# Two weight loads of a cached-attention decode kernel: a quarter of each as 8-row loads from GpSimd's queue to partitions 64 to 127

## The chip, the cores and the metric

The kernel runs on one core of a Trainium2 chip. The metric is device microseconds of one execution; the time of a version is the median of its runs. Everything is in 32-bit floats.

## The reference

Two layers, each a grouped-query attention over a long cache for one new token, followed by a small mixer over the channels; the same weights and the same cache serve both layers. Two batch rows, 32 query heads on 8 key/value heads, 32,768 cached positions, head size 128.

```python
q = (x @ wq)...                                   # x: (2, 1, 512) after a layer norm
scores = jnp.einsum("bhqd,bhkd->bhqk", q, k) * (Dh ** -0.5)
p = _softmax(scores, axis=-1)
o = jnp.einsum("bhqk,bhkd->bhqd", p, v)
...
x = x + _A_ref(_layernorm(x), k_cache, v_cache, wq, wo)
x = x + _B_ref(_layernorm(x), w1, b1, w2, b2)     # mixer: b2 + w2 . gelu(w1 * norm + b1) on each channel
x = x + _A_ref(_layernorm(x), k_cache, v_cache, wq, wo)
x = x + _B_ref(_layernorm(x), w1, b1, w2, b2)
```

## The kernel before

A unit is one (layer, batch row, key/value head): 32 units, each with 8 chunks of K and 8 of V, 2 MB a chunk. For each unit TensorE forms the scores of its four query heads against K (L426), ScalarE the exponentials (L466), and TensorE the weighted sums of V (L581). One key/value head is a "keeper": much of its cache stays in memory from layer 0 to layer 1.

All of K, V and the weights come through SyncE's queue into one large tile, `mem`, cut into 13 cells of 16 KB a partition and a rest of five slots of 2 KB. Cells 0 to 8 (0 to 10 around the change of layer) hold K and V in a ring, cells 9 to 12 hold weights. A list of loads, `stream`, sorted by key, sets the order of the loads and of the matmuls; one step of it is one chunk. The function `at(time, f, ...)` hangs other work on steps of this stream: `make_q` some 6 steps ahead of a unit's K, `load_weights` 10 ahead, and so on. SyncE issues a load when the buffer's last readers and its last load are done, and each engine runs its own list of instructions in order.

Weights are loaded for two heads at once: `wqo[k]` holds for each partition the four query tiles (512 columns each, one for each block of 128 input channels `d`) and the four output tiles of both heads, 4 MB. `load_weights` (L115 to 118) brings them as one load of 128 rows; seven such loads are in the program, and the pair with number 1 (heads 2 and 3) is loaded twice, once in each layer. `q_products` (L340) multiplies the normalised input `xnT[:, d]` with query tile `d`, four products for each query, all into one bank.

`spot()` (L302) hands out scratch slots of 512 columns, eight of them in turn, all in cell 8. GpSimd computes a power now and then (L271, L685, L871) and issues no load.

Of the kernel before, what the change touches and what calls it, by code (L numbers as in the profile page):

```python
# [13 lines left out]
P = 128  # L14
CK = 4096
# [5 lines left out]
RING = 3  # L21
# [7 lines left out]
REST = 5  # L29
IN_PSUM = (4, 5, 3)  # L30
KEPT_Q = 4
RESIDENT = (5, 7)
TWO_HEADS = ((0, 1), (2, 3), (4, 6), RESIDENT)
FOLLOWS = {2: (2.2, -0.9, -0.8, -0.7, 3.5, -0.6, -0.5, -0.4), 5: (3.05, 0.1, 0.2, 0.3, 5.1, 3.1, 3.2, 3.3)}
PIECES = (32, 16, 8, 4, 4)
THIN = 16
QT = 4
# [7 lines left out]
def gqa_mixer_kernel(ctx: ExitStack, tc: tile.TileContext, x, kt, v, wqo, cols, out):  # L45
# [17 lines left out]
    nc = tc.nc  # L63
    B, D = out.shape
# [4 lines left out]
    R = wqo.shape[2] // (4 * D)  # L69
    DT = D // P  # L70
    FT = (cols.shape[1] - 1) // 4
# [13 lines left out]

    NP = 28 + 32 * 2
    widths = dict(x=B * DT, xn=B * DT, q=KEPT_Q * R, cols=4 * FT + 1, ident=P, one=1, half=1, selg=R * QT)
    widths |= dict(selh=R, mask=QT, others=B, oz=2 * R * B, qpads=NP, unit=2 * 16, ln=16 + 2 * FT)
    small_sb = const.tile([P, sum(widths.values())], F32, name="small_sb")
    sm, w0 = {}, 0  # L90
    for name, w in widths.items():
# [6 lines left out]
    W = wqo.shape[2] // 4  # L98
    assert CK == 2 * W
    WCELL0, WCELLS = RING * RING, 4  # L100
    heads = list(range(HKV))
    passing = [h for h in heads if h not in RESIDENT]
    home = {}
    mem = const.tile([P, (WCELL0 + WCELLS) * CK + REST * QT * DH], F32, name="mem")

    def cells(k, m=1):
        return mem[:, k * CK : (k + m) * CK]

    def wq_at(h):
        return cells(home[h])[:, :W].rearrange("p (t c) -> p t c", t=DT)  # L110

    def wo_at(h):
        return cells(home[h])[:, W:].rearrange("p (t c) -> p t c", t=R)

    def load_weights(k, cell):  # L115
        for j in range(2):
            home[TWO_HEADS[k][j]] = cell + j
        nc.sync.dma_start(cells(cell, 2), wqo[k])


    busy = [0] * 2 * (WCELL0 + WCELLS + 1)
    now = [0]
# [72 lines left out]
    ident = sm["ident"]  # L195
# [31 lines left out]
    rows = kept[-1]  # L227
# [52 lines left out]
    N1 = len(units) - 1  # L280
# [5 lines left out]
    N3 = len(units) - 1  # L286
# [7 lines left out]
    xnT = sm["xn"].rearrange("p (d b) -> p d b", b=B)  # L294
# [5 lines left out]
    spots = [0]  # L300

    def spot():  # L302

        spots[0] += 1
        return cells(RING * RING - 1)[:, spots[0] % (CK // D) * D :][:, :D]

    def to_columns(key):

# [24 lines left out]
    def q_products(n, *ds):  # L333

        layer, b, h = unit_of(n)
        m = 1 if partner(n) is None else B
        for d in ds:
            if d == 0:
                q_ps[n] = bcast if N1 < n <= N3 + 2 else kept[0]
            nc.tensor.matmul(  # L340
                q_ps[n][:m, :],
                xnT[:, d, b : b + m],
                wq_at(h)[:, d, :],
                start=(d == 0),
                stop=(d == DT - 1),
            )

    def make_q(n, step, place=None):

# [339 lines left out]
    ln = sm["ln"]  # L689
# [52 lines left out]
    def last_mixer(n):  # L742
# [185 lines left out]
    kbeg, k_done, vbeg, v_done, vend_of, v_from, v_to, brings, starts, t = {}, {}, {}, {}, {}, {}, {}, [], [], 0  # L928
# [13 lines left out]
    def at(time, f, *a, rank=1):  # L942
        done.setdefault(time, []).append((rank, f, a))

    HC = NCH // HALVES
    opens = {two[0]: k for k, two in enumerate(TWO_HEADS)}
    mixed = {}
    for n in range(NU):
        layer, b, h = unit_of(n)
# [19 lines left out]
                assert max(v_done[n - 2, c] for c in range(HC)) <= q2  # L969
        if n and h in opens and (units[n] == (0, 0, h) or h in passing and units[n] == (1, 0, h)):  # L970
            at(kbeg[n] - (7 if n == N3 + 2 else 10), load_weights, opens[h], WCELL0 + opens[h] % 2 * 2)
        if n in (N1 + 1, N2 + 1):
            at(kend - 0.5, turn_scores, n, 0, rank=2)
            at(kend, q_products, n + 1, 0)
            at(kend, max_1, n)
            at(kend, q_products, n + 1, 1)
            at(kend, max_2, n)
            at(kend, exponentials_at_once, n, 0)
            at(kend, q_products, n + 1, 2, 3)
            t1 = kend + 2  # L980
            assert mixed[units[n - 1][:2]] == kend == kbeg[n + 1] - 2
            at(t1, turn_scores, n, 1, rank=2)
            at(t1, exponentials_at_once, n, 1, rank=2)
            at(t1 + 1, sums, n)
            assert t1 + 1 < v_done[n, HC] - 1
        else:
            t1 = max(kend + 2, ahead + (2 if urgent else 4))
            e = kend if N1 < n <= N3 else kend + 2
            at(max(kend, e - 1), max_1, n)
            at(e, max_2, n)  # L990
            t0 = max(k_done[n, HC - 1], *(v_done[n - 1, c] for c in range(HC) if n), 0)
            if n in (N2, N3):
                t0 = max(t0, kbeg[n + 1] - 3)
            at(t0, turn_scores, n, 0)
            at(e, exponentials, n, 0)
            if n == NU - 1:
                t1 = ahead
                assert t1 >= kend + 2 and vbeg[n] == ahead
            at(t1, turn_scores, n, 1)
            at(t1, exponentials, n, 1)  # L1000
# [74 lines left out]
    t = 0  # L1075
# [11 lines left out]
    assert not done, sorted(done)  # L1087


def _layout(A_x, A_k_cache, A_v_cache, A_wq, A_wo, B_w1, B_b1, B_w2, B_b2):  # L1090

    import numpy as np

    B, HKV, SK, DH = A_k_cache.shape
    D = A_x.shape[-1]
    n = SK // CK


    keys = np.arange(SK).reshape(n, CK)
    for c0, m in GROUPS:  # L1100
        keys[c0 : c0 + m] = keys[c0 : c0 + m].reshape(P, m, CK // P).transpose(1, 0, 2).reshape(m, CK)
    k = keys.reshape(n // PACK, PACK // 2, 2, NG, 32, JT // QT, QT // SUB, SUB)
# [11 lines left out]
    return {  # L1114
        "x": np.ascontiguousarray(A_x.reshape(B * (D // P), P).T),
        "kt": kt,
        "v": A_v_cache.reshape(B * HKV, SK * DH),
        "wqo": np.stack([np.concatenate([wqo[h] for h in two], axis=1) for two in TWO_HEADS]),
        "cols": np.concatenate(cols, axis=1),
    }  # L1120

# [24 lines left out]
```

## Time and profile before

| | us |
|---|---|
| median of 3 runs (lowest to highest) | 2491.31 (2490.64 to 2491.49) |
| the profiled execution, its own time | 2490.09 |
| its span | 2488.0 |
| TensorE busy | 1371.4 (55%) |
| VectorE, ScalarE, GpSimd busy | 244.9, 187.7, 4.9 |
| bytes read from HBM | 1061.19 MB, 427 GB/s over the span |

The profile page cuts the span into 40 slices of 62.2 us; its DMA row gives the busy share of the 16 DMA engines in tenths, its GB/s row what they moved. Section 3 lists queues: q1 is SyncE's, q10 ScalarE's, q8 and q14 fetch instructions and tables. A table of stretches gives for each stretch the busy time of each engine, then the granted share of TensorE's clock, the DMA share (the mean over 16 engines; packets count where they are recorded, so single rows can pass 1.00) and GB/s. No view names a single DMA engine.

### The profile page before, as it was taken

How to read it: one execution, taken by the hardware profiler on the slowest of the kernel's cores; microseconds unless marked ns; L12 is line 12 of the kernel's file. 1: busy time of each engine (PE TensorE's matmuls, PEld its weight loads, DVE VectorE, ACT ScalarE, POOL GpSimd, SP SyncE). 2: the span in 40 equal slices, each digit the busy share in tenths (PEclk: the TensorE clock that was granted, in tenths of full speed). 3: DMA queues.
4: the chain of work that ended last, by engine and by line, in shares of the span. 5: the costliest groups of instructions: out<-in, count | busy, mean ns of one | idle time of the engine just before them, and what ended most of it. 6: DMA issues, size and time to landing. Idle time of an engine off the chain costs nothing.

```text
span 2488.0 us, 20543 instructions
## 1 busy us (share of the span) xinstructions
PE 1371.4 (55%) x9302; PEld 376.2 (15%) x9302; DVE 244.9 (10%) x643; ACT 187.7 (8%) x554; POOL 4.9 (0%) x17
## 2 busy tenths in 40 slices
PE   4544445544545454657677665455455465455546
PEld 1111111111111111111121121111111111111112
DVE  1000000000000000003113110000000000010002
ACT  0000000000000000002012000000000000011002
POOL 0000000000000000000000000000000000000000
PEclk8777767876777777778888887777678677777878
DMA  9999999999999999999999999999999999999996
GB/s 421 437 432 428 433 436 430 434 435 427 436 436 432 426 436 431 427 431 407 433 427 417 428 432 432 438 430 431 432 428 438 428 429 435 431 434 431 432 431 291
DMA packets 30336, 1062.51 MB, mean 427 GB/s; under 512 B 3621, under 2 KB 3625, under 8 KB 4266
## 3 DMA queue, kind: packets, MB, share of 16 engines
q1 hardware_dynamic: 29960, 1061.17, 99.1%
q8 instruction: 73, 1.20, 0.2%
q14 instruction: 13, 0.11, 0.0%
q10 hardware_dynamic: 290, 0.04, 0.0%
HBM read 1061.19 MB, written 0.00 MB: 427 GB/s over the span
## 4 chain that ended last, share of the span: by engine, by line
DMA 73%; PE 25%; DVE 1%; issue 0%; another core or an unknown queue 0%; ACT 0%; SPq 0%; POOL 0%; ACTq 0%
DMA mem<-in_v_dram 64%; PE acc L581 20%; DMA mem<-in_kt_dram 9%; PE scores L426 3%; PE small L612 0%; PE small L455 0%; PE small L449 0%; PE bcast L340 0%; ACT S L466 0%; PE small L642 0%; PE kept L246 0%; PE kept L792 0%; PE bcast L672 0%; DVE S L551 0%
## 5 line engine op out<-in xcount | busy, mean ns | idle before, releaser
L426 PE MATMUL scores<-mem,small_sb 128*32 128x512 f32 x4096 | 631.7, 736 | 605.4 <-DMA mem<-in_kt_dram 605.2
L581 PE MATMUL acc<-mem,S 128*16 128x512 f32 x4088 | 596.8, 723 | 457.1 <-DMA mem<-in_v_dram 447.7
L426 PEld LDWEIGHTS scores<-mem,small_sb 128*32 128x32 f32 x4096 | 150.0, 129 | 988.7 <-issue 903.7
L466 ACT ACTIVATE S<-S,small_sb 128x128 f32<-128x128 f32 x240 | 123.4, 517 | 2107.9 <-DVE small_sb L457 1556.9
L581 PEld LDWEIGHTS acc<-mem,S 128*16 128x16 f32 x4088 | 132.6, 109 | 810.8 <-issue 664.4
L441 DVE TENSOR_REDUCE small_sb<-scores 128x1 f32<-128x512 f32 x64 | 44.2, 691 | 819.5 <-PE scores L426 819.5
L461 DVE STREAM_TRANSPOSE S<-scores 128x512 f32<-128x512 f32 x64 | 45.5, 710 | 116.0 <-PE acc L581 116.0
L340 PE MATMUL kept<-mem,small_sb 128*2 128x512 f32 x104 | 51.1, 617 | 1.7 <-DVE small_sb L274 1.7
L466 ACT ACTIVATION_READ_ACCUMULATOR S<-S,small_sb 128x1 f32 x240 | 44.7, 186 | 0.0
L246 PE MATMUL kept<-mem,small_sb 128*1 128x512 f32 (+1 forms) x236 | 42.4, 598 | 2.6 <-ACT mem L835 2.4
L451 DVE TENSOR_REDUCE small_sb<-small 1x4 f32<-1x128 f32 x32 | 8.9, 279 | 277.7 <-PE small L449 277.7
L614 DVE RECIPROCAL small_sb<-small 128x4 f32<-128x4 f32 x32 | 5.9, 185 | 304.6 <-PE small L612 304.6
L623 DVE TENSOR_TENSOR small_sb<-small,small_sb 128x4 f32<-128x4 f32 x31 | 5.1, 164 | 295.8 <-PE small L621 295.8
L551 DVE SCALAR_TENSOR_TENSOR S<-acc,small_sb,S 128x128 f32<-128x128 f32 x93 | 32.6, 351 | 3.3
L835 ACT ACTIVATE S<-bcast,small_sb 128x512 f32<-128x512 f32 x28 | 21.5, 777 | 87.2 <-DVE small_sb L704 85.1
L366 PE MATMUL small<-small_sb,mem 2*128 2x2 f32 x112 | 15.5, 256 | 17.9 <-DVE mem L362 17.9
L549 DVE TENSOR_SCALAR S<-acc,small_sb 128x128 f32<-128x128 f32 x31 | 10.8, 350 | 147.3 <-PE acc L581 147.3
L621 PEld LDWEIGHTS small<-small_sb,S 128*128 128x128 f32 x62 | 12.7, 258 | 48.8 <-issue 41.2
L340 PE MATMUL bcast<-mem,small_sb 128*1 128x512 f32 (+1 forms) x40 | 19.4, 600 | 0.0
L366 PEld LDWEIGHTS small<-small_sb,mem 2*128 2x128 f32 x112 | 14.3, 196 | 30.5 <-DVE mem L362 27.3
L852 DVE SCALAR_TENSOR_TENSOR acc<-S,small_sb,acc 128x512 f32<-128x512 f32 x24 | 18.1, 755 | 2.5
L449 PE MATMUL small<-small_sb 128*1 128x128 f32 x64 | 16.6, 353 | 3.1 <-DVE small_sb L447 3.1
(147 smaller groups left out, 285.3 us busy)
## 6 DMA issues: line engine op xcount, KB each, us to landing
mem<-in_kt_dram SPq DMA_DIRECT2D x14, 4096.0 KB, 22.5
mem<-in_v_dram SPq DMA_DIRECT2D x11, 4096.0 KB, 29.2
mem<-in_wqo_dram SPq DMA_DIRECT2D x7, 4096.0 KB, 37.6
mem<-in_v_dram SPq DMA_DIRECT2D x13, 2048.0 KB, 21.3
mem<-in_kt_dram SPq DMA_DIRECT2D x12, 2048.0 KB, 19.3
mem<-in_kt_dram SPq DMA_DIRECT2D x24, 1024.0 KB, 8.8
mem<-in_v_dram SPq DMA_DIRECT2D x21, 1024.0 KB, 8.8
mem<-in_kt_dram SPq DMA_DIRECT2D x2, 6144.0 KB, 24.2
```

Source lines behind the costliest of these rows:

```text
L246: nc.tensor.matmul((rows if to is None else to)[32 * g : 32 * g + b + 1, :], weights if b else weights[:, 1:], row, start=to is not None, ...
L340: nc.tensor.matmul(q_ps[n][:m, :], xnT[:, d, b : b + m], wq_at(h)[:, d, :], start=(d == 0), stop=(d == DT - 1),)
L366: nc.tensor.matmul(pt[:, r * m : (r + 1) * m], q_row[n][:m, r * DH : (r + 1) * DH], ident[:m, :m], start=True, stop=True,)
L426: nc.tensor.matmul(sc_ps[n, half][32 * g : 32 * g + 32, :], q, kc[k * NG + g], start=(i == 0 and k == 0), stop=(i == PACK - 1 and k == SUB ...
L441: nc.vector.tensor_reduce(mx[n][:, half : half + 1], sc_ps[n, half], axis=AX.X, op=ALU.max)
L449: nc.tensor.matmul(pm[:1, :P], mxa, ident, start=True, stop=True)
L461: nc.vector.transpose(S[half], sc_ps[n, half])
L466: nc.scalar.activation(s[:, :, h], s[:, :, h], AF.Exp, bias=neg[n][:, h : h + 1], scale=SCALE, accum_out=lsum[n][:, half, h : h + 1],)
L551: nc.vector.scalar_tensor_tensor(t, acc[:, k * DH : (k + 1) * DH], mask[:, k : k + 1], t, op0=ALU.mult, op1=ALU.add)
L581: nc.tensor.matmul(acc[32 * g : 32 * g + R * QT, :], S[half][:, col : col + R * QT], vc[q], start=(c == v_from[n] and q < NG), stop=(c == ...
L835: nc.scalar.activation(hid[key, f], px[key], AF.Gelu_apprx_tanh, bias=shift[key][:, f : f + 1], scale=slope[key][:, f : f + 1],)
L852: nc.vector.scalar_tensor_tensor(h if f == FT - 1 else acc, h, w, acc, op0=ALU.mult, op1=ALU.add)
```

## The change

For the pair with number 1, `UPPER`, the last two query tiles of both heads (`RAISED = 2`, the tiles for `d` = 2 and 3) leave the main load, which becomes 3 MB. They are laid out in HBM as tiles of 64 rows: rows 64 to 127 of the weights and, beside them, rows 0 to 63. `raise_tiles` loads both into partitions 64 to 127 of cell 8, 16 KB a partition, 1 MB in all, by eight loads from GpSimd's queue. Load `r` takes eight partitions that lie 4 apart, from `64 + r % 4 + 32 * (r // 4)`; each row is two runs of 8 KB. Behind each of them GpSimd issues a tiny load of 8 rows with two single elements each, into a new field `step` that nothing reads; VectorE clears that field first.

`raise_input` copies, by a product with the identity and a copy on VectorE, the parts of the input for channels 256 to 319 and 384 to 447 to partitions 64 to 127. `q_products` then forms for each raised tile two products over 64 rows in place of one over 128.

Both steps are hung 28 steps ahead of the unit's K. Because cell 8 now holds the raised tiles outside the middle of the program, `spot()` uses the five slots of the rest there, and cell 8 as before from the first step of unit `N1` to that of unit `N3 + 4`.

```diff
+    def load_weights(k, cell):
+        tiles = 2 * (DT + R - RAISED * (k == UPPER))
...
+        of = wqo[k].rearrange("p c -> (p c)")[: P * tiles * D].rearrange("(p c) -> p c", p=P)
+        nc.sync.dma_start(mem[:, cell * CK :][:, : tiles * D], of)
+
+    def raise_tiles():
+        to = mem[H:, (WCELL0 - 1) * CK :][:, : 4 * RAISED * D].rearrange("u (i c) -> u i c", i=2)
...
+        of = wqo[UPPER].rearrange("p c -> (p c)")[-H * 4 * RAISED * D :].rearrange("(i u c) -> u i c", i=2, u=H)
+        nc.vector.memset(sm["step"], 0.0)
+        for r in range(8):
+            u = r % 4 + H // 2 * (r // 4)
+            i = steps[0] % 16
+            steps[0] += 1
+            step = nc.gpsimd.dma_start, sm["step"][i::16, ::2], cols[i::16, :3:2]
+            rows = nc.gpsimd.dma_start, to[u : u + 29 : 4], of[u : u + 29 : 4]
+            for f, *a in (rows, step):
+                f(*a)
+
+    def raise_input():
+        p = misc()
+        nc.tensor.matmul(p[H:, : RAISED * B], ident[:, :H], sm["xn"][:, -RAISED * B :], start=True, stop=True)
+        nc.vector.tensor_copy(sm["up"][H:, :], p[H:, : RAISED * B])
...
     def spot():
-        return cells(RING * RING - 1)[:, spots[0] % (CK // D) * D :][:, :D]
+        inside = kbeg[N1] <= now[0] < kbeg[N3 + 4]
+        w, m = ((WCELL0 - 1) * CK, CK // D) if inside else ((WCELL0 + WCELLS) * CK, REST)
+        return mem[:, w + spots[0] % m * D :][:, :D]
...
     def q_products(n, *ds):
-            nc.tensor.matmul(
-                q_ps[n][:m, :],
-                xnT[:, d, b : b + m],
-                wq_at(h)[:, d, :],
-                start=(d == 0),
-                stop=(d == DT - 1),
-            )
+            j = d - (DT - RAISED)
+            if h in raised and j >= 0:
+                up = sm["up"][:, j * B : (j + 1) * B]
+                pairs = [(x[H:, b : b + m], t) for x, t in zip((xnT[:, d, :], up), raised[h][j])]
+            else:
+                pairs = [(xnT[:, d, b : b + m], wq_at(h, d))]
+            for i, (x, t) in enumerate(pairs):
+                nc.tensor.matmul(
+                    q_ps[n][:m, :], x, t, start=(d == 0), stop=(d == DT - 1 and i == len(pairs) - 1)
+                )
...
             at(kbeg[n] - (7 if n == N3 + 2 else 10), load_weights, opens[h], WCELL0 + opens[h] % 2 * 2)
+            if opens[h] == UPPER:
+                at(kbeg[n] - 28, raise_tiles)
+                at(kbeg[n] - 28, raise_input)
```

GpSimd's list before, from its power in the first input to the one in the first mixer (`TENSOR_TENSOR`); in brackets the semaphores that an instruction waits for:

```order
L220 MEMSET small_sb 128x92
L271 TENSOR_TENSOR mem<-mem,small_sb 128x2 [waits DVE_49,Pool_49]
L685 TENSOR_TENSOR small_sb<-small_sb 128x1 [waits DVE_49]
L871 TENSOR_TENSOR small_sb<-small_sb 128x1 [waits DVE_49]
L685 TENSOR_TENSOR small_sb<-small_sb 128x1 [waits DVE_49]
```

The same place after, from the first power to the sixth row load (L144 with `mem` is a row load, with `small_sb` a tiny one):

```order
L303 TENSOR_TENSOR mem<-mem,small_sb 128x2 [waits DVE_49,Pool_49]
L144 DMA mem<-in_wqo_dram 8x2x2048
L144 DMA small_sb<-in_cols_dram 8x2x1 [waits DVE_49]
L144 DMA mem<-in_wqo_dram 8x2x2048
L144 DMA small_sb<-in_cols_dram 8x2x1
L144 DMA mem<-in_wqo_dram 8x2x2048
L144 DMA small_sb<-in_cols_dram 8x2x1
L144 DMA mem<-in_wqo_dram 8x2x2048
L144 DMA small_sb<-in_cols_dram 8x2x1
L144 DMA mem<-in_wqo_dram 8x2x2048 [waits DMASW0_49]
L144 DMA small_sb<-in_cols_dram 8x2x1 [waits DMASW1_49]
L144 DMA mem<-in_wqo_dram 8x2x2048 [waits DMASW2_49]
```

Sixteen loads stand between two powers that followed one another. The first row load waits for nothing, the first tiny one for VectorE, and from the fifth row load on each waits for the load four pairs ahead of it.

VectorE's list after, at the place where the field is cleared (`MEMSET`) and the input raised (`COPY` to 64 partitions):

```order
L478 TENSOR_REDUCE small_sb<-scores 128x1
L498 STREAM_TRANSPOSE S_91<-scores 128x512
L136 MEMSET small_sb 128x3
L150 COPY small_sb<-small 64x4
L648 TENSOR_TENSOR small_sb<-small_sb 128x4
L651 RECIPROCAL small_sb<-small 128x4
```

Before, the transpose (L461 there) was followed by the addition of the sums (L611) at once.

More of the change, by code (lines that the diff above doesn't have):

```diff
@@ L33 @@
 TWO_HEADS = ((0, 1), (2, 3), (4, 6), RESIDENT)
+UPPER, RAISED = 1, 2
 FOLLOWS = {2: (2.2, -0.9, -0.8, -0.7, 3.5, -0.6, -0.5, -0.4), 5: (3.05, 0.1, 0.2, 0.3, 5.1, 3.1, 3.2, 3.3)}
@@ L87, in gqa_mixer_kernel @@
     widths = dict(x=B * DT, xn=B * DT, q=KEPT_Q * R, cols=4 * FT + 1, ident=P, one=1, half=1, selg=R * QT)
-    widths |= dict(selh=R, mask=QT, others=B, oz=2 * R * B, qpads=NP, unit=2 * 16, ln=16 + 2 * FT)
+    widths |= dict(selh=R, mask=QT, others=B, oz=2 * R * B, qpads=NP, unit=2 * 16, ln=16 + 2 * FT, step=3, up=RAISED * B)
     small_sb = const.tile([P, sum(widths.values())], F32, name="small_sb")
@@ L107, in cells, with wq_at @@
         return mem[:, k * CK : (k + m) * CK]
-    def wq_at(h):
-        return cells(home[h])[:, :W].rearrange("p (t c) -> p t c", t=DT)
+    H = P // 2
+    raised = {}
+    def wq_at(h, d):
+        return mem[:, home[h] + d * D :][:, :D]
     def wo_at(h):
-        return cells(home[h])[:, W:].rearrange("p (t c) -> p t c", t=R)
+        w = home[h] + (DT - RAISED * (h in raised)) * D
+        return mem[:, w : w + W].rearrange("p (t c) -> p t c", t=R)
     def load_weights(k, cell):
+        tiles = 2 * (DT + R - RAISED * (k == UPPER))
         for j in range(2):
-            home[TWO_HEADS[k][j]] = cell + j
-        nc.sync.dma_start(cells(cell, 2), wqo[k])
+            home[TWO_HEADS[k][j]] = cell * CK + j * (tiles // 2) * D
+        of = wqo[k].rearrange("p c -> (p c)")[: P * tiles * D].rearrange("(p c) -> p c", p=P)
+        nc.sync.dma_start(mem[:, cell * CK :][:, : tiles * D], of)
+    steps = [0]
+    def raise_tiles():
+        to = mem[H:, (WCELL0 - 1) * CK :][:, : 4 * RAISED * D].rearrange("u (i c) -> u i c", i=2)
+        for j in range(2):
+            raised[TWO_HEADS[UPPER][j]] = [[to[:, i, (RAISED * j + d) * D :][:, :D] for i in range(2)] for d in range(RAISED)]
+        of = wqo[UPPER].rearrange("p c -> (p c)")[-H * 4 * RAISED * D :].rearrange("(i u c) -> u i c", i=2, u=H)
[12 more added lines that the diff above has]
+        nc.vector.tensor_copy(sm["up"][H:, :], p[H:, : RAISED * B])
     busy = [0] * 2 * (WCELL0 + WCELLS + 1)
@@ L1087, in gqa_mixer_kernel, with _two_heads @@
     assert not done, sorted(done)
+def _two_heads(two, parted, d):
+    import numpy as np
+    if not parted:
+        return np.concatenate(two, axis=1)
+    c = np.arange((d // P - RAISED) * d, d // P * d)
+    main = np.concatenate([np.delete(a, c, axis=1) for a in two], axis=1)
+    top = [np.concatenate([a[u : u + P // 2, c] for a in two], axis=1) for u in (P // 2, 0)]
+    return np.concatenate([a.ravel() for a in (main, *top)]).reshape(P, -1)
 def _layout(A_x, A_k_cache, A_v_cache, A_wq, A_wo, B_w1, B_b1, B_w2, B_b2):
@@ L1117, in _layout @@
         "v": A_v_cache.reshape(B * HKV, SK * DH),
-        "wqo": np.stack([np.concatenate([wqo[h] for h in two], axis=1) for two in TWO_HEADS]),
+        "wqo": np.stack([_two_heads([wqo[h] for h in two], k == UPPER, D) for k, two in enumerate(TWO_HEADS)]),
         "cols": np.concatenate(cols, axis=1),
```

## The prediction

> **What bounds the kernel now.** I read the page from the top: first the span and the slices, then the queues, then the chain.
>
> ```profile
> span 2488.0 us, 20543 instructions
> ...
> DMA  9999999999999999999999999999999999999996
> GB/s 421 437 432 428 433 436 430 434 435 427 436 436 432 426 436 431 427 431 407 433 427 417 428 432 432 438 430 431 432 428 438 428 429 435 431 434 431 432 431 291
> ...
> q1 hardware_dynamic: 29960, 1061.17, 99.1%
> q8 instruction: 73, 1.20, 0.2%
> ...
> q10 hardware_dynamic: 290, 0.04, 0.0%
> ...
> DMA 73%; PE 25%; DVE 1%; issue 0%; another core or an unknown queue 0%; ACT 0%; SPq 0%; POOL 0%; ACTq 0%
> ```
>
> The 16 DMA engines carry packets for 99.1% of the span, all from SyncE's queue (q1). A typical slice moves 432 GB/s, which is 27.0 GB/s for each engine. So time is bytes: 64 KB on one engine costs 65,536 / 27.0 = 2.43 us, and 128 KB 4.85 us. The change moves no byte away from the kernel. It can only win where some engines stand still while others work. Two views show such places. The first is the table of stretches at the very end of the loads (the last two columns are the DMA share and GB/s):
>
> ```profile
> 2464.00:2465.00 1.00, 1.00 (x12) 0.13 (x4) 0.00 (x0) 0.00 (x0) 0.00 (x0) 1.00 0.97 403
> 2465.00:2466.00 1.00, 0.25 (x4) 0.00 (x0) 0.00 (x0) 0.00 (x0) 0.00 (x0) 1.00 0.95 383
> 2466.00:2467.00 1.00, 0.57 (x8) 0.25 (x12) 0.00 (x0) 0.00 (x0) 0.00 (x0) 1.00 0.92 367
> 2467.00:2468.00 1.00, 1.00 (x16) 0.12 (x4) 0.00 (x0) 0.00 (x0) 0.00 (x0) 1.00 0.59 240
> 2468.00:2469.00 1.00, 0.44 (x8) 0.10 (x8) 0.00 (x0) 0.00 (x0) 0.00 (x0) 1.00 0.48 193
> 2469.00:2470.00 1.00, 0.95 (x8) 0.03 (x6) 0.00 (x0) 0.00 (x0) 0.00 (x0) 1.00 0.48 188
> 2470.00:2471.00 1.00, 0.80 (x24) 0.43 (x24) 0.91 (x3) 0.00 (x0) 0.00 (x0) 1.00 0.33 123
> 2471.00:2472.00 1.00, 0.76 (x18) 0.31 (x10) 0.56 (x3) 0.00 (x0) 0.00 (x0) 1.00 0.08 16
> ```
>
> Full, then a plateau at 0.48 for two rows, then nothing: half of the engines end at about 2467.3, the other half at about 2470.6. I call them the leading and the lagging half; at the end they are 3.3 us apart. The eight shares add up to 4.80, so with even work the last byte would land at 2468.8 instead of about 2471: 2.2 us earlier.
>
> The second place is the change of layer, in stretches of 10 us:
>
> ```profile
> 1110.00:1120.00 10.00, 2.90 (x28) 1.33 (x24) 1.64 (x4) 3.62 (x10) 0.00 (x0) 0.89 0.90 388
> 1120.00:1130.00 10.00, 7.11 (x42) 1.74 (x46) 2.06 (x4) 0.00 (x0) 0.00 (x0) 0.60 1.04 441
> 1130.00:1140.00 10.00, 5.21 (x44) 1.17 (x40) 0.00 (x0) 0.00 (x0) 0.00 (x0) 0.91 0.97 410
> 1140.00:1150.00 10.00, 8.90 (x70) 2.75 (x62) 1.82 (x6) 0.00 (x0) 0.00 (x0) 0.92 0.95 382
> 1150.00:1160.00 10.00, 5.27 (x38) 1.14 (x42) 6.53 (x13) 5.40 (x8) 0.54 (x1) 1.00 1.00 384
> ```
>
> Against 432 GB/s these five rows lack 44, −9, 22, 50 and 48, together 155, which is 3.6 us of all engines. SyncE has little queued there, and engines that are ahead run dry. No view names an engine, so that it is the leading half which runs dry is my reading of the 0.48 plateau.
>
> What makes a half lag? Of what the queues show, the instruction fetches (q8) are the likeliest: 0.2% of 16 x 2488 us is 80 us of engine time, 73 packets of 16 KB, 1.09 us each. On eight engines that would be 10 us each over the run, enough for the 3.3 us at the end and for the dry spells.
>
> **The change part by part.** The two main loads shrink from 4 to 3 MB, so each engine saves 64 KB, 2.43 us, per load. The missing 1 MB comes as eight loads of 8 rows, 16 KB a row. If one such load sits on eight engines, one row each, and always on the same eight, these get 128 KB, 4.85 us, per load. Net, per load: +2.43 us on the eight that take the rows, −2.43 us on the other eight.
>
> Where do the loads stand in time?
>
> ```profile
> 218.77 0.43 SPq L118 DMA_DIRECT2D mem<-in_wqo_dram  x1
> ...
> 1723.94 0.42 SPq L118 DMA_DIRECT2D mem<-in_wqo_dram  x1
> ```
>
> The first is far ahead of the change of layer, the second 750 us before the end. So each can level one of the two places. If the rows fall to the leading half:
>
> - First load, change of layer: the lagging half arrives 2.43 us earlier. The gain is between 0 (the stretch is set by computing) and 2.43. The 3.6 us of idle engine time there speak for the upper part; I take 1.9.
> - Second load, end: the lagging half ends 2.43 earlier; the leading half, 3.3 ahead, gets 2.43 more and would be 2.43 − 3.3 + 2.43 = 1.6 us last if nothing else moved, a gain of 3.3 − 2.43 = 0.9. If the leading half spends its extra bytes where it was dry anyway, the gain is the full 2.43. I take 1.6.
>
> The small packets: each tiny load puts two 4-byte elements on each of its engines, and every load has completions. Per weight load that is some 16 elements on each engine of one half, and 16 completions on all. The nearest row is q10, 290 small packets at 0.0%, under 0.05% of 39,808 us, so under 0.07 us each: 0 to 1.1 us for the elements per load and as much for the completions. 3,621 packets under 512 B are lost in the main stream without a trace in its rate, so I take 0.15 per load, 0.3 in all.
>
> GpSimd now issues 32 DMAs. Its own work is next to nothing, and it mostly waits:
>
> ```profile
> PE 1371.4 (55%) x9302; PEld 376.2 (15%) x9302; DVE 244.9 (10%) x643; ACT 187.7 (8%) x554; POOL 4.9 (0%) x17
> ...
> POOL small_sb L685 <- DVE small_sb L702: 2173.6, 3, 1136.0
> ```
>
> Its next computing instruction behind the first group is the power at the change of layer (the 0.54 us on POOL in 1150 to 1160 above), some 900 us later; behind the second group the one at the end of layer 1. The group's second instruction waits for a clearing on VectorE that stands behind the transpose of this row, and from the fifth row load on each waits for an earlier load to land. The rows are needed where the query products of heads 2 and 3 stand:
>
> ```profile
> 161.57 0.70 DVE L461 STREAM_TRANSPOSE S<-scores 128x512 f32<-128x512 f32 x1
> ...
> 282.14 1.45 PE L340 MATMUL kept<-mem,small_sb 128*2 128x512 f32 x3
> ```
>
> That leaves 282 − 162 = 120 us for 16 short loads. An 8 MB load lands 28.6 us after issue:
>
> ```profile
> mem<-in_kt_dram SPq DMA_DIRECT2D x48, 28.6
> ...
> L340 PE MATMUL kept<-mem,small_sb 128*2 128x512 f32 x104 | 51.1, 617 | 1.7 <-DVE small_sb L274 1.7
> ```
>
> Even at 28.6 us for each round of four row loads, two rounds are 57 us. If that cover were gone, TensorE would stand at the query product and scores behind it would hold up buffers, but the slack is 60 us. TensorE gets two more products for each of four queries, 8 x 0.617 = 4.9 us, and two copies of the input; it is 55% busy and waits for DMA in these stretches, so I cost that at nothing. The scratch slots that move into five places instead of eight I cost at nothing too: each is read one step after it is written.
>
> Sum: −1.9 − 1.6 + 0.3 = −3.2 us. The profiled execution took 2490.09 us, 2.1 around its span, and lies 1.22 under the median of the runs; 2490.09 − 3.2 = 2486.9, and as a median 2488.1.
>
> [...]
>
> **The rivals.**
>
> *Slower: the rows fall to the lagging half.* Place: the engines that take the 8-row loads. Nothing in the code says which half the first row load meets. Price: +2.43 us on the half that ends last, twice, and 0.3: +5.2, 2496.5. It decides as soon as the eight engines are the lagging ones; there is no slack, since that half has no idle time to put them in. For it: the rows go to partitions 64 to 127, and it is open whether their own engines lead. Against it: the shift is just of the size that the lag calls for.
>
> *The destination counts, not the engine.* Partitions 64 to 127 now get 64 KB more per eight of them and load, partitions 0 to 63 as much less. If writing into one set of partitions has a limit near the 27.0 GB/s of an engine, the rows stand in the way of the engines that serve that set: +2.43 per load for the later side, +4.9 and 0.3, 2496.5. The main stream cannot tell, for it loads all partitions evenly. [...]
>
> *Row packets cost more than their bytes.* The only 16 KB packets from another queue are the fetches, 1.09 us against 0.61 at the stream's rate. At that price a load's rows cost 8 x 1.09 = 8.7 us on their engines, net +6.3; that half, 3.3 ahead, then ends 3.0 late, twice: +6.0, 2497.3. For it: the row of q8. Against it: those packets do not go to the partitions, and q10's small ones cost nothing visible.
>
> *No shift.* Each 8-row load spreads over all engines, or lands now on one half and now on the other: +0.3, 2491.6.
>
> **How the numbers follow.** Chances: forecast 0.42, rows on the lagging half 0.20, the destination 0.15, dear packets 0.12, no shift 0.08, something else 0.03. The forecast's own range is 2486.4 (the full 2 x 2.43) to 2490.3 (1 us gained). For 8 in 10 the range must take in both +5 rivals: 2486.4 to 2497.4. The bound of 0.2%, about what a measurement of this kernel can tell from no change, is 5.0 us: 2486.3 to 2496.3. The forecast gives 0.08 of its chance beyond it, the two rivals at +5.2 lie across the upper bound and give half each (0.175), dear packets nearly all (0.12), the rest and the unknown 0.055. So faster 0.08, same 0.57, slower 0.35.
>
> **What would show it.** Right: a new software queue with about 2 MB and some hundreds of packets; the plateau near 0.5 at the end shorter than 2 us; stretches at the change of layer above their present 382 to 410 GB/s. Rows on the lagging half: the plateau grows to 5 us or more. The destination or dear packets: GB/s falls under 425 in the slices around 165 to 250 and 1640 to 1760 us, where it is 428 to 433 now. Late rows: TensorE waits for the new queue ahead of a query product. The forecast is wrong if the time is above 2491.3 or if the plateau does not shrink.

## The result, and the profile after

| | before | after |
|---|---|---|
| median of the runs (lowest to highest), us | 2491.07 (2490.64 to 2491.49) | 2514.19 (2512.51 to 2517.81) |
| ratio to before, 95% interval | | 1.0095 (1.0077 to 1.0112) |
| span of the profiled execution, us | 2488.0 | 2510.1 |

The changed kernel is 23.1 us slower, almost 1%. The forecast was 2488.1 with a range up to 2497.4; the time lies far outside. The page of the changed kernel, its span, slices and queues:

```profile
span 2510.1 us, 20635 instructions
...
DMA  9999999999999999999999999999999999999996
GB/s 420 433 422 403 422 434 433 426 433 435 432 434 430 433 434 431 428 428 396 434 425 416 428 426 434 435 423 396 406 433 434 433 432 433 431 434 432 430 432 281
...
q1 hardware_dynamic: 29960, 1059.08, 98.7%
q0 software_dynamic: 1280, 2.10, 0.3%
q8 instruction: 73, 1.20, 0.2%
```

A slice is now 62.75 us. The third to fifth (125 to 314 us) fell to 422, 403 and 422 GB/s, and the slices from 1631 to 1820 to 423, 396 and 406. Those are the times of the two groups of row loads, but for the first load of each group. The DMA row still shows 9: the engines are not idle there, they are slow. The queues say the same. SyncE's packets took 98.7% of 2510.1 us, 2477.5 us an engine, for 2 MB less than before; before it was 99.1% of 2488.0, 2465.6 us (the shares are rounded, so each figure is good to 1.3 us).

The first group closer, in stretches of 20 us (the last two columns are DMA share and GB/s). Before:

```profile
160.00:180.00 20.00, 9.70 (x78) 2.25 (x66) 2.38 (x5) 2.11 (x8) 0.00 (x0) 0.83 1.00 433
180.00:200.00 20.00, 8.95 (x64) 2.47 (x64) 0.88 (x3) 0.00 (x0) 0.00 (x0) 0.74 0.97 420
200.00:220.00 20.00, 10.12 (x68) 2.81 (x68) 1.84 (x6) 2.18 (x8) 0.00 (x0) 0.74 1.01 436
220.00:240.00 20.00, 9.68 (x74) 2.65 (x74) 1.48 (x3) 1.25 (x5) 0.00 (x0) 0.83 1.02 440
240.00:260.00 20.00, 9.34 (x66) 2.29 (x66) 1.07 (x3) 0.86 (x4) 0.00 (x0) 0.74 0.99 429
```

After, the same stretches:

```profile
160.00:180.00 20.00, 10.90 (x80) 2.71 (x72) 1.85 (x6) 2.11 (x8) 2.27 (x4) 0.74 1.01 414
180.00:200.00 20.00, 7.74 (x64) 2.23 (x60) 0.72 (x1) 0.00 (x0) 1.69 (x3) 0.74 1.00 401
200.00:220.00 20.00, 6.21 (x42) 1.59 (x37) 1.16 (x4) 0.00 (x0) 1.70 (x3) 0.66 0.99 403
220.00:240.00 20.00, 9.00 (x64) 2.31 (x56) 1.57 (x5) 2.18 (x8) 1.69 (x3) 0.75 1.05 416
240.00:260.00 20.00, 8.19 (x70) 2.21 (x73) 1.65 (x4) 2.11 (x8) 1.12 (x2) 0.76 0.93 379
```

The mean falls from 432 to 403 GB/s, at a DMA share of 1.00 in both. Row bytes are counted in the 403. In these 100 us alone 29/432 of the time, 6.7 us, goes.

The packet records of the traces, which the views do not print one by one, say which packets are slow. The 64 KB packets of the main stream that start from 160 to 260 us took 2.43 us on average before and 2.58 in the changed kernel; from 1680 to 1772 us it was 2.42 against 2.65. Their extra time, shared among 16 engines, is 5.6 us in the first stretch and 7.3 in the second: 12.9 us of the loss stand there.

The end of the loads, which the prediction read for the two halves:

```profile
2486.00:2487.00 1.00, 1.00 (x16) 0.21 (x8) 0.00 (x0) 0.00 (x0) 0.00 (x0) 1.00 0.97 387
2487.00:2488.00 1.00, 0.52 (x8) 0.00 (x0) 0.00 (x0) 0.00 (x0) 0.00 (x0) 1.00 0.70 277
2488.00:2489.00 1.00, 0.53 (x8) 0.22 (x12) 0.00 (x0) 0.00 (x0) 0.00 (x0) 1.00 0.50 201
2489.00:2490.00 1.00, 1.00 (x16) 0.15 (x8) 0.00 (x0) 0.00 (x0) 0.00 (x0) 1.00 0.50 193
2490.00:2491.00 1.00, 0.46 (x8) 0.08 (x8) 0.00 (x0) 0.00 (x0) 0.00 (x0) 1.00 0.27 102
2491.00:2492.00 1.00, 0.98 (x8) 0.06 (x8) 0.00 (x0) 0.00 (x0) 0.00 (x0) 1.00 0.23 80
2492.00:2493.00 1.00, 0.74 (x22) 0.43 (x24) 0.88 (x3) 0.00 (x0) 0.00 (x0) 1.00 0.06 23
```

The plateau at 0.50 did not shrink. Half of the engines end near 2487.5, some four more near 2490, the last near 2492. It now has two steps and is some 5 us long, far from the 23 us that are lost: the loss is not at the end.

At the change of layer, now some 10 us later:

```profile
1120.00:1130.00 10.00, 1.31 (x16) 0.12 (x4) 0.46 (x2) 3.62 (x10) 0.00 (x0) 0.72 0.92 395
1130.00:1140.00 10.00, 9.34 (x66) 2.25 (x66) 2.07 (x4) 0.00 (x0) 0.00 (x0) 0.77 1.06 450
1140.00:1150.00 10.00, 3.15 (x20) 0.66 (x20) 0.00 (x0) 0.00 (x0) 0.00 (x0) 0.74 0.95 401
1150.00:1160.00 10.00, 8.87 (x70) 2.70 (x62) 1.85 (x6) 0.00 (x0) 0.00 (x0) 0.92 0.91 365
1160.00:1170.00 10.00, 5.63 (x38) 1.26 (x42) 6.50 (x13) 5.39 (x8) 0.57 (x1) 0.94 1.00 393
```

Against 432 these lack 37, −18, 31, 67 and 39, together 156, where the five rows before lacked 155. Nothing was won there.

What held up the query products (L381 now), of the groups of the changed kernel:

```profile
L381 PE MATMUL kept<-mem,small_sb 128*2 128x512 f32 (+1 forms) x120 | 57.8, 612 | 1.7 <-DVE small_sb L306 1.7
```

As before, 1.7 us for VectorE and none for a DMA: the rows were not late.

### The profile page after: what moved, and what is told of

It is laid out like the page before. It is cut to its first block, busy times and chain, and to the rows that moved or that the text cites. A ratio compares the mean times of both kernels' runs of the same rounds, so it can differ in the third digit from the quotient of the medians.

```text
span 2510.1 us, 20635 instructions
## 1 busy us (share of the span) xinstructions
PE 1381.0 (55%) x9322; PEld 375.4 (15%) x9322; DVE 245.5 (10%) x647; ACT 188.1 (7%) x554; POOL 23.2 (1%) x49
## 3 DMA queue, kind: packets, MB, share of 16 engines
q1 hardware_dynamic: 29960, 1059.08, 98.7%
## 4 chain that ended last, share of the span: by engine, by line
DMA 74%; PE 24%; issue 0%; another core or an unknown queue 0%; DVE 0%; ACT 0%; SPq 0%
DMA mem<-in_v_dram 65%; PE acc L618 19%; DMA mem<-in_kt_dram 9%; PE scores L463 3%; PE small L492 0%; PE small L649 0%; PE bcast L381 0%; PE small L486 0%; PE kept L278 0%; PE kept L829 0%; PE small L679 0%; PE bcast L733 0%; DVE S L588 0%; PE bcast L709 0%
## 5 line engine op out<-in xcount | busy, mean ns | idle before, releaser
L463 PE MATMUL scores<-mem,small_sb 128*32 128x512 f32 x4096 | 621.0, 728 | 607.6 <-DMA mem<-in_kt_dram 607.6
L618 PE MATMUL acc<-mem,S 128*16 128x512 f32 x4088 | 604.4, 732 | 467.6 <-DMA mem<-in_v_dram 462.1
L381 PE MATMUL kept<-mem,small_sb 128*2 128x512 f32 (+1 forms) x120 | 57.8, 612 | 1.7 <-DVE small_sb L306 1.7
L381 PE MATMUL bcast<-mem,small_sb 128*1 128x512 f32 (+1 forms) x40 | 21.4, 652 | 0.0
L658 PEld LDWEIGHTS small<-small_sb,S 128*128 128x128 f32 x62 | 12.7, 255 | 48.5 <-issue 40.9
## 6 DMA issues: line engine op xcount, KB each, us to landing
mem<-in_kt_dram SPq DMA_DIRECT2D x14, 4096.0 KB, 23.1
```

What stands on the lines that cost most here:

```text
L381: nc.tensor.matmul(q_ps[n][:m, :], x, t, start=(d == 0), stop=(d == DT - 1 and i == len(pairs) - 1))
L463: nc.tensor.matmul(sc_ps[n, half][32 * g : 32 * g + 32, :], q, kc[k * NG + g], start=(i == 0 and k == 0), stop=(i == PACK - 1 and k == SUB ...
L618: nc.tensor.matmul(acc[32 * g : 32 * g + R * QT, :], S[half][:, col : col + R * QT], vc[q], start=(c == v_from[n] and q < NG), stop=(c == ...
```

## The experiments

Three theories stood at the start. **D**: the destination counts. Eight engines write rows into partitions that other engines are filling. **P**: packets of a second queue are dear wherever they go. **T**: the tiny loads and the completions cost it. Ratios are to the kernel before, run on the same chip. Two words are used below: the *collision* is what it costs when one set of eight engines writes rows into the partitions that the other set fills; the *shift* is what it costs that one set carries 2.43 us more per load and the other as much less.

### Where do the rows go, and do the tiny loads matter?

**low**: the tiles in partitions 0 to 63, everything else as in the changed kernel.

```diff
-        to = mem[H:, ...
+        to = mem[:H, ...
...
-    ... ident[:, :H] ... p[H:, ...] ... sm["up"][H:, :]
+    ... ident[:, H:] ... p[:H, ...] ... sm["up"][:H, :]
...
-                pairs = [(x[H:, b : b + m], t) ...
+                pairs = [(x[:H, b : b + m], t) ...
...
-    ... for u in (P // 2, 0)]
+    ... for u in (0, P // 2)]
```

> The row loads, the tiny loads and the doubled products stay; the raised tiles lie in partitions 0 to 63 instead of 64 to 127, and the input is moved accordingly. Theory D (destination): the 23 us are lost because eight engines write rows into partitions that other engines are filling from the main stream; then the place decides, and with the rows on the same eight engines but in the other half of the partitions the loss is mostly gone: 2486 to 2500. Theory P (dear packets): an 8 KB packet of a second queue costs its engine far more than its bytes wherever it goes: 2510 to 2518, as in the changed kernel. Theory T (the tiny loads and the completions cost it): 2510 to 2518 too.

Measured: 2499.91 us, ratio 1.0034 (1.0022 to 1.0046). Its first group, in the stretches shown above:

```profile
160.00:180.00 20.00, 9.43 (x68) 2.37 (x68) 2.46 (x7) 2.11 (x8) 2.27 (x4) 0.74 1.01 436
180.00:200.00 20.00, 8.88 (x64) 2.52 (x64) 0.81 (x3) 0.00 (x0) 1.69 (x3) 0.74 1.00 430
200.00:220.00 20.00, 9.11 (x68) 2.59 (x68) 0.52 (x3) 2.19 (x8) 2.26 (x4) 0.74 1.02 441
220.00:240.00 20.00, 9.08 (x70) 2.53 (x70) 1.57 (x5) 0.00 (x0) 1.69 (x3) 0.74 1.01 435
240.00:260.00 20.00, 9.79 (x78) 2.46 (x73) 1.66 (x4) 2.11 (x8) 0.56 (x1) 0.74 1.00 429
```

The mean is back at 434 GB/s with the same loads, the same queue and the same packets. The 64 KB packets of the two stretches are back at 2.43 us on average, and the row packets of 160 to 260 us took 0.31 us where the changed kernel's took 0.36. The place of the destination alone is worth 14.3 us between the two medians, or 14.8 with each taken against the kernel before on its own chip. P and T fall as the main cause; 8 us stay to be explained.

**no_tiny**: without the tiny loads and the clearing.

```diff
-        nc.vector.memset(sm["step"], 0.0)
...
-            for f, *a in (rows, step):
+            for f, *a in (rows,):
```

> The changed kernel without the sixteen tiny loads and the clearing ahead of them; the sixteen row loads go to partitions 64 to 127 as before. Theory T (tiny loads and completions): most of the 23 us go, under 2495. Theory D (destination) and theory P (dear packets): the rows cost what they cost, 2508 to 2518, if they still sit on the same eight engines. If without the tiny loads the rows fall on both sets of eight by turns, D expects about half of the loss (2500 to 2506), since half of the rows are then written by the engines that fill these partitions anyway, and P still the whole of it, spread over all engines.

Measured: 2500.45 us, 1.0038 (1.0025 to 1.0052). Taken alone this looks like theory T. I followed the packet records one behind another (here an engine's next packet starts within some 5 ns of the end of its last). Here each of the sixteen engines took seven to nine of the 128 row packets of the first group, where in the changed kernel eight engines took all of them. So the tiny loads keep the rows on one set of eight, and without them the sets take turns. D's second case, 2500 to 2506, is the one that fits. The rows also move at another time here: with no clearing to wait for, GpSimd issues them from 17 and 1443 us on, where all but the first of each group came from 164 and 1679 us on in the changed kernel.

**tiny_only**: the kernel before with eight tiny loads ahead of each of the two weight loads, no rows.

```diff
...
+            nc.gpsimd.dma_start(sm["step"][i::16, ::2], cols[i::16, :3:2])
```

> The kernel before, with the whole 4 MB weight loads from SyncE's queue, and eight tiny loads from GpSimd's queue ahead of each of the two loads of pair 1: no rows. Theory T: a large part of the 23 us, 2500 to 2514. Theories D and P: the time of the kernel before, 2490 to 2492.5.

Measured: 2491.39 us, 1.0001 (0.9992 to 1.0011), which is −2.0 to +2.7 us. T is out as the main cause.

**sp_rows**: the eight row loads from SyncE's queue, no tiny ones.

```diff
-            rows = nc.gpsimd.dma_start, to[...
+            rows = nc.sync.dma_start, to[...
```

> The eight row loads of each weight load are issued by SyncE into its own queue, without tiny loads, still to partitions 64 to 127. Theory D: the destination is the same, so if the rows sit on eight engines that do not fill these partitions the loss stays, 2505 to 2518; on engines that do, or spread over all sixteen, it falls with the share. Theory P in its form of two queues that alternate on an engine: no second queue, so 2490 to 2497. Theory P in its form of a dear 8 KB packet: 2505 to 2518.

Measured: 2503.27 us, 1.0049 (1.0033 to 1.0066). It separates nothing. SyncE's list shows why, with its waits from 120 to 170 us and the table of stretches behind it:

```profile
124.90 27.95 SPq L143 DMA_DIRECT2D mem<-in_wqo_dram  x8
```

```profile
SPq L143 <- DMA mem<-in_kt_dram: 20.6, 1, 20.6
```

```profile
145.00:150.00 5.00, 0.00 (x0) 0.00 (x0) 0.00 (x0) 0.00 (x0) 0.00 (x0) 0.50 0.78 272
```

From the first of the eight short loads to the last SyncE took 28 us, 20.6 of them in one wait for an earlier load of K to land. The next large load was issued behind them, at 153 us, and engines stood idle (0.78, 272 GB/s): a cost of its own that hides the one asked for.

### Is it the destination, or the pair of engine and destination?

**swap** puts the tiny load first, so that the rows meet the other eight engines; **low_swap** is the same with low tiles.

```diff
-            for f, *a in (rows, step):
+            for f, *a in (step, rows):
```

> The changed kernel with the two loads of each pair in the other order: the tiny load first, the row load behind it. Without the tiny loads the rows went to both sets of eight engines by turns, so this order should put all rows on the other eight engines; the destination stays at partitions 64 to 127. Theory D in the form of pairs (an engine collides when it writes partitions that the other eight engines fill): these eight fill partitions 64 to 127 themselves, so the collision of about 14 us is gone and what is left is the shift of bytes between the halves, about as with the tiles in partitions 0 to 63: 2497 to 2504. A rival, that any row load into partitions 64 to 127 is slow, whichever engine brings it: 2510 to 2518. If the engines did not change: 2514 too, and the trace shows it by 64 KB packets that are slowed as before.

> The tiles in partitions 0 to 63 and the tiny load ahead of the row load: the other eight engines write partitions 0 to 63. Theory D in the form of pairs: now they collide with the eight engines that fill these partitions: 2508 to 2518. The rival that only partitions 64 to 127 are slow: 2497 to 2504, as with the other order.

Measured: swap 2500.32 us, 1.0033 (1.0020 to 1.0046); low_swap 2518.31 us, 1.0107 (1.0092 to 1.0122), just above its range. With the two kernels above this makes a square:

| us over before, same chip | tiles in 64 to 127 | tiles in 0 to 63 |
|---|---|---|
| row load first | 23.1 | 8.3 |
| tiny load first | 9.0 | 27.0 |

Neither the engines nor the partitions cost it by themselves, but the crossing: 14.3 us (the changed kernel less low) to 18.0 (low_swap less swap). The 64 KB packets bear it out: from 160 to 260 us they took 2.58 and 2.63 us on average in the two kernels that cross (the changed kernel and low_swap), and 2.43 in the two that do not (low and swap). Theory D holds in its form of pairs. By the square the two sets have each their half of the partitions, and a row that is brought by an engine of one set into the half of the other is the dear one: 14.3 to 18.0 us for the 256 row packets of a kernel.

### The collision and the shift apart

**even** was meant to have neither: rows of one run of 8 KB, sixteen loads by turns to the two halves, in the layout of the kernel before; **even_cross** turns the destinations round.

```diff
...
+        for r in range(16):
+            u = r // 2 % 4 + H // 2 * (r // 8) + H * (r % 2)        # even_cross: H * (1 - r % 2)
+            nc.gpsimd.dma_start(to[u : u + 29 : 4], of[u : u + 29 : 4])
```

> No shift and, by theory D, no collision: the same 1 MB of each weight load comes by sixteen loads of 8 rows of 8 KB from GpSimd's queue, without tiny loads, by turns to partitions 0 to 63 and 64 to 127, so that each set of eight engines writes the partitions that it fills anyway; the query products are the ones of the kernel before. Theory D with the shift as the second cost: neither is left, 2490 to 2494. Theory P (packets of a second queue cost something by themselves): 2496 or more.

> As the even kernel, but by turns to partitions 64 to 127 and 0 to 63, so that each set of eight engines writes the partitions of the other set: collision without shift. Theory D: the collision alone. The changed kernel lost 14.3 us more than the one with its tiles in partitions 0 to 63, for the same rows: 2502 to 2509. If the collision counts for little without the shift: under 2496.

Measured: even 2504.58 us, 1.0055 (1.0040 to 1.0070); even_cross 2505.25 us, 1.0059 (1.0042 to 1.0076). The expectation for even missed. Its packet records show why: as far as they can be linked, the rows were all on one set of eight engines, some sixteen each, so that both kernels have the full shift and half of the collision. They lost 13.2 and 13.9 us; shift (3.8 to 6.4) and half a collision (7.2), as sized below, make 12.7 to 15.3 with the 1.7 us of the turns kernel. So even_cross fell into its expected range by luck: it was not the collision without shift that it was meant to be. The rows of no_tiny, two runs each, had gone to both sets by turns (seven to nine of 128 packets on each engine); why these stayed on one set was not shown.

**turns** and **turns_cross**: the same once more with rows of two runs of 4 KB.

```diff
-        to = mem[:, (WCELL0 - 1) * CK :][:, : 2 * RAISED * D]
+        to = mem[:, (WCELL0 - 1) * CK :][:, :CK].rearrange("p (j c) -> p j c", j=2)[:, :, : RAISED * D]
```

> The even kernel again, which kept its rows on one set of eight engines, now with rows of two runs of 4 KB (the tiles of the second head lie 8 KB further in cell 8). The row loads of two runs a row in the kernel without tiny loads went to both sets by turns; if these do too, each set writes the partitions that it fills anyway, with as many bytes on each. Theory D with the shift as the second cost: neither is left, 2490 to 2494. If packets of a second queue cost something by themselves: 2496 or more. If the rows stay on one set: 2503 to 2506, as in the even kernel.

> As the turns kernel, but by turns to partitions 64 to 127 and 0 to 63: all rows collide, without a shift. Theory D: the price of the collision alone, 14 to 18 us by the differences of the changed kernel to the one with low tiles (14.3) and of the two kernels with the tiny load first (18.0): 2503 to 2510. If the rows stay on one set: as the turns kernel.

Measured: turns 2492.93 us, 1.0008 (0.9999 to 1.0018); turns_cross 2507.53 us, 1.0063 (1.0048 to 1.0078). Three stretches with rows in turns:

```profile
20.00:40.00 20.00, 10.92 (x54) 3.24 (x55) 0.91 (x3) 0.00 (x0) 1.12 (x2) 0.74 1.01 433
40.00:60.00 20.00, 9.99 (x84) 2.66 (x80) 1.37 (x3) 0.00 (x0) 1.66 (x3) 0.74 0.99 427
60.00:80.00 20.00, 7.35 (x46) 2.19 (x38) 1.13 (x3) 0.00 (x0) 1.66 (x3) 0.66 1.00 429
```

And in turns_cross:

```profile
20.00:40.00 20.00, 10.85 (x58) 3.20 (x59) 0.91 (x3) 0.00 (x0) 1.12 (x2) 0.74 0.96 381
40.00:60.00 20.00, 7.72 (x52) 1.77 (x48) 1.37 (x3) 0.00 (x0) 1.66 (x3) 0.68 1.05 427
60.00:80.00 20.00, 7.49 (x60) 1.91 (x53) 0.85 (x2) 0.00 (x0) 1.65 (x3) 0.67 0.94 379
```

433, 427, 429 against 381, 427, 379 GB/s: the two programs have the same loads, the same bytes on both sets and the same products, and differ only in which set writes which half. As far as the packet records can be linked, each of the 16 engines took about 16 of the 256 row packets of the first group in both. The 64 KB packets that start from 20 to 130 us took 2.42 us on average in turns and 2.59 in turns_cross. The collision alone is 14.6 us. Rows from GpSimd's queue without collision and shift are near nothing (1.7 us, and the interval, −0.2 to 4.5, holds no change): little or nothing is left for P.

### What are the 8 us without a collision?

**struct** has the products, the raised input and the scratch slots of the change, but the whole main load. Each raised tile is formed from rows 64 to 127 twice, so rows 0 to 63 of these tiles are left out of the sum.

```diff
+            if h in raised and d >= 2:
+                pairs = [(x[H:], w[H:]), (sm["up"][H:, (d - 2) * B :][:, b : b + m], w[H:])]
```

> No bytes are moved: the whole 4 MB main load of the kernel before, but the eight further products, the raised input, the two copies and the five scratch slots of the changed kernel. Each raised tile is formed from rows 64 to 127 twice, so rows 0 to 63 of these tiles are left out of the sum. The prediction costed all this at nothing: 2490.5 to 2493. If the products or the slots hold up the stream: 2494 or more, and part of the 8 to 9 us of the kernels without collision is theirs.

**low_1** halves the shift.

```diff
-UPPER, RAISED = 1, 2
+UPPER, RAISED = 1, 1
```

> The kernel with the tiles in partitions 0 to 63, with one query tile of each head raised instead of two (RAISED = 1): half the bytes shifted, 64 KB on each of the eight engines and 1.21 us less main load on all, per weight load; no collision. If the cost of the shift is in proportion to its bytes: half of 8.3, 2494 to 2497. If the lead of the eight engines, some 1.2 us at the first load, pays for a shift of that size, as the prediction's sum for two tiles assumed: 2489.5 to 2492.

Measured: struct 2494.42 us, 1.0012 (1.0002 to 1.0021); low_1 2495.88 us, 1.0017 (1.0008 to 1.0027). So there is a cost of the structure, 3.2 us here, and low_1 with half the shift loses 4.6 us where low lost 8.3 and, in its second run below, 6.9: between half and two thirds. It has half of the further products too, so its shift can't be taken out exactly. The four below were run on one chip, in five rounds, to part the two; **spots** is the kernel before with the five scratch slots, and **struct_2**, **low_2**, **swap_2** repeat kernels.

> The structure without moved bytes again (rows 0 to 63 of the raised tiles left out of the sum), with more rounds, beside the kernels with a shift and no collision on the same chip. If the structure costs some 3 us, as its first run gave: 2493 to 2496, and the shift would be its bytes, 4.85 us for both loads. If it costs nothing: 2490.5 to 2492, and the shift costs 8 us or more, almost twice its bytes.

> The kernel before with one thing of the change: scratch goes round five slots of the rest in place of eight of cell 8. If the structure's cost lies in waits for these slots: 2493 to 2496, like the whole structure. If it lies in the further products or nowhere: 2490.5 to 2492.

> The kernel with low tiles again, shift without collision: 2498 to 2501 as in its first run. The shift's own price is its difference to the structure: 4.85 us if each load costs the 2.43 us by which one set of eight engines is longer than before and no engine's lead pays for any of it; under 3 us if a lead pays for part.

> The shift to the other eight engines, without collision, again. If one set of eight had a usable lead of 3.3 us, as the prediction read from the plateau, the two kernels with a shift would differ by up to twice that; by the view that no lead can be kept they are equal: 2498 to 2501 both.

| | us | ratio, interval |
|---|---|---|
| struct_2 | 2494.25 | 1.0011 (1.0002 to 1.0020) |
| spots | 2491.01 | 0.9997 (0.9989 to 1.0006) |
| low_2 | 2498.03 | 1.0025 (1.0015 to 1.0036) |
| swap_2 | 2500.63 | 1.0039 (1.0026 to 1.0051) |

The structure costs 3.1 us here; its interval is wide, 0.5 to 5.0 us. The slots cost nothing that shows (−2.7 to 1.5 us). The shift is what is left: 2498.03 − 2494.25 = 3.8 us for low, 2500.63 − 2494.25 = 6.4 for swap, around the 4.85 that two loads cost when one set has 2.43 us more to carry and no lead pays for it. The profile shows the shift as engines that stand still behind the second group. Stretches 1780 to 1820 of before:

```profile
1780.00:1800.00 20.00, 14.33 (x80) 4.36 (x80) 1.57 (x5) 0.00 (x0) 0.00 (x0) 0.76 1.01 427
1800.00:1820.00 20.00, 9.62 (x72) 2.78 (x76) 1.85 (x6) 2.19 (x8) 0.00 (x0) 0.76 0.99 426
```

of low (its first run):

```profile
1780.00:1800.00 20.00, 12.97 (x64) 3.08 (x68) 0.00 (x0) 0.00 (x0) 0.00 (x0) 0.72 0.97 420
1800.00:1820.00 20.00, 13.02 (x92) 4.10 (x84) 3.41 (x11) 2.18 (x8) 0.00 (x0) 0.83 0.92 387
```

and of swap (its first run):

```profile
1780.00:1800.00 20.00, 11.31 (x56) 2.81 (x57) 0.00 (x0) 0.00 (x0) 0.00 (x0) 0.64 0.94 404
1800.00:1820.00 20.00, 14.43 (x98) 4.35 (x95) 3.41 (x11) 2.19 (x8) 0.00 (x0) 0.91 0.88 368
```

Here the DMA share falls, to 0.92 and 0.88, unlike in the stretches of the collision above. That is (7 + 39)/432 x 20 = 2.1 us in the one and (23 + 58)/432 x 20 = 3.8 us in the other. The second runs of both show the dip in the same place, less deep in swap's. That the set without rows waits there for the set with rows is my reading, and no view shows it. For it: in the trace of before the sixteen completions of a load lie 3.4 us apart from first to last (median), the 171 waits of TensorE that ended within 0.4 us of a completion all ended behind the sixteenth, and SyncE issues the next load when the readers of a buffer are through.

## Why the prediction was wrong

The whole, put together from differences of medians: structure 3.1 (struct_2), shift 3.8 to 6.4 (low_2 and swap_2 less struct_2), collision 14.6 (turns_cross less turns), together 21.5 to 24.1; measured 23.1. None of the three was taken from the changed kernel's own time.

- **What bounds the kernel** held: bytes on the DMA engines. TensorE never waited for the rows.
- **Rows on one set of eight, all of them**, was an assumption, for the trace of before holds no load from GpSimd. It was right, as far as the packet records can be linked: eight engines took all row packets of the first group. That the set is the one which leads at the end was not shown. The rival "no shift" falls with this; turns, where the rows went to both sets, lost 1.7 us.
- **The cost of the rows at their bytes, 4.85 us a load** is the term that failed. The price came from the rate of the stream, 27.0 GB/s an engine, which the main stream reaches where no rows cross. Where the rows did not cross either it held: in low a row packet took 0.31 us, against 0.30 at that rate. The rival "the destination counts, not the engine" named the mechanism and the slices in which it would show, but was sized by the same rate: +5.2 us in place of 23. That put its end of the range at 2496.5. Measured, the collision is 7.2 us a load and 14.3 in all (the changed kernel less low), and most of it lies not on the rows but on the 64 KB packets that run beside them (12.9 us of extra time in the two stretches above). The time of SyncE's packets bears it out: low's page (span, then its queues) gives 98.6% of 2498.7 us, 2463.7 us an engine for the same bytes, against 2477.5, each good to 1.3 us.

```profile
span 2498.7 us, 20636 instructions
...
q1 hardware_dynamic: 29960, 1059.08, 98.6%
q0 software_dynamic: 1280, 2.10, 0.2%
```

- **The gain from the shift, 1.9 + 1.6 us**, has the wrong sign. The step that failed is the reading of the plateau at the end, 3.3 us, as a lead that one half holds and could spend. Shifted to the one set or to the other, without collision, the kernel got slower: by 8.3 and 6.9 us in the two runs of low, by 9.0 and 9.5 in the two of swap. Had one set a usable lead of 3.3 us, the two would have differed by up to 6.6; they differ by 0.7 and 2.6. The first of these pairs ran on two chips, the second on one; its 2.6 us leave room for a small lead, but not for a gain. The structure taken off, the shift costs 3.8 to 6.4 us. That is near the 4.9 us that the rival "the rows fall to the lagging half" asked for, whichever set carries the rows. What makes half of the engines end later was not tested.
- **TensorE's further products and the scratch slots at nothing** was 3.1 us off for the whole structure (interval 0.5 to 5.0). By spots the slots are hardly it; the products and the raised input were not parted. Which wait of SyncE or of TensorE it is stays open; no single stretch of the profile shows it.
- **Small packets 0.3 us** and **GpSimd's waits at nothing** held for the tiny loads within −2.0 to +2.7 us: 2491.39 against 2491.64 us for tiny_only.
- **Dear packets** (a second queue's packets cost more than their bytes wherever they go): refuted as a cost of this size by turns and by low's 434 GB/s.
- **The range** failed with the price: the two rivals at +5.2 us came from the one rate of the stream, taken as exact, and the third, at +6.0, from the fetch packets. None priced what a row does to the packets of other engines, so the range ended at 2497.4. Its lower end, 2486.4, left out the 0.3 us of the small packets, which changes nothing here.

None of the kernels beat the one before; turns, which moves the same bytes by GpSimd's queue, is level with it within its interval.

## What to carry to other kernels

A rate read from a stream in which nothing crosses is no price for a load that does (here 4.85 us a load by that rate, and 7.2 more for the crossing): before moving bytes to "the free half", find out which engines serve which partitions, and test the crossing with the two destinations swapped. A lag between engines at the end of a profile need not be a reserve in the middle of it: here 3.3 us of lag bought nothing. And when several rivals are sized by the same number, widen the range for that number.

## What the runs showed of the hardware

- A row of two 8 KB runs brought into partitions that the other eight engines were filling cost far more than its own bytes. The changed kernel has 256 such packets and lost 14.3 us on 16 engines: 14.3 x 16 / 256 = 0.89 us of engine time for each, on top of the 0.30 us that 8 KB take at 27.0 GB/s. In turns_cross 512 packets of 4 KB lost 14.6 us, 0.46 us each: between these two it goes by bytes.
- The delay falls mostly on the packets of the main stream, and on both sets: from 160 to 260 us of the changed kernel the 64 KB packets took 2.57 us on average where a row packet could be linked to the engine and 2.60 where none could, against 2.43 before; its row packets took 0.36 us against 0.31 in low.
- Loads of 8 rows of two runs took turns between the two sets of eight engines when nothing lay between them (no_tiny: seven to nine of 128 row packets on each of the sixteen), and stayed on one set with a tiny 8-row load between (the changed kernel: eight engines took all). Loads of 8 rows of one run stayed on one set without it (even: some sixteen packets on each of eight); why was not tried.
